# State products taken batch by batch in the layer's layout, and half of a folded weight summed by slices of its contraction

## The chip, the cores and the metric

The kernel runs on one core of one Trainium2 chip. Its metric is the device time of that core in microseconds (us).

## The reference, cut to what matters

```python
# x: (8, 8, 512, 64), state: (8, 8, 32, 64): B, H, S, D and Ns = 32
a     = softmax(scale * x @ state.T)      # over the 32 states
xread = a @ state                         # (B, H, S, D): "x reads state"
a2    = softmax(scale * state @ x.T)      # over the 512 positions
sread = a2 @ x                            # (B, H, Ns, D)
x = concat([xread, sread], axis=2)        # 8 * 544 = 4352 tokens of 512
x = ((x @ w1) * (x @ w2) @ w3) @ w_out    # d_ff 1024, w1 w2 w3 w_out in f64
y = ((x @ wa) * (x @ wb)) @ wo2           # d_ff 1536, the output, f32
```

## The kernel before, in words

The weights come in f64. `load64` brings a raw tile of 512 KB as 32-bit words, and `Convert` makes f32 of it: two ACT activations, a DVE shift and an add on POOL for each raw tile. The SBUF is used as 47 units of 4 KB per partition, and PSUM as 8 banks of 128x512 f32. Products at full width are made in three passes of the f32r type (`PASSES`): every operand is split into a high part (a cast on ACT) and a low part (a subtraction on DVE or POOL), and high x high, high x low and low x high are added in PSUM.

Two products of weights replace work on tokens. First, `w3 @ w_out` is folded once into one 1024x512 weight, `ws`: for each of its eight row blocks, `w3` is loaded by rows, converted, transposed on PE (`transpose_w3`, tiles `w3t`), split and multiplied (`weight_product`, 24 matmuls into a bank `wp`). Second, since xread = a @ state, layer 1 multiplies the attention weights with P = state @ (w1 | w2) of each batch, whose contraction has 256 rows. `state_product` makes P for four batches at once: a matmul takes 64 rows (one head of a pair, r = 0 or 1), 128 columns of the transposed state (4 batches x 32 states) and 512 columns of one of the eight converted weight tiles `wk{p}_{nh}`. Its 64 matmuls fill banks `pb`, ACT or DVE copy them to units `sg` (`product_move`), and `product_store` writes them to DRAM `p_d` in the layer's layout. `load_p` brings one of four chunks of a batch back (`pr`, 512 KB), and `split_p` makes its high part `ph` (ACT) and low part `pl` (POOL, two halves).

The early phase has no order by hand: every operation is a Job with an engine, an estimated time, predecessors and a priority, and `run_jobs` puts them in an order greedily by those estimates; `EARLY` is the order of the loads. In it stand the weight conversions, the folded weight, the attention of batch 0, the state products, and all of layer 1 for batch 0 (`first_product`, tile `f`; `first_output`, tile `x2f`).

Then `block1` runs batches 1 to 7, eight steps `f` each. A step issues on PE: `ap` (6 matmuls) with its copy on ACT; the middle fills; `bp` (6) with the multiplication on DVE and the split into `hp`; the behind fills; and the 12 `x2p` matmuls of the step before. The fills hold the attention of the next batch at fixed steps (`scores` at step 1, for example). The banks in rotation are four, since four more hold the `x2p` sums. The 256 state rows ("s") run interleaved with batch 7, with w1 and w2 loaded a second time by columns (`sw`, 16 loads of 512 KB, and their conversions). Layer 2 (`block2`) follows and isn't touched.

Of the kernel before, what the change touches and what calls it, by code (L numbers as in the profile page):

```python
# [9 lines left out]
F32 = mybir.dt.float32  # L10
F32R = mybir.dt.float32r
# [13 lines left out]
    "wo1 wo3 wo0 w3_1 wo2 w3_2 w3_0 wk0_0 x0 wk1_0 wk2_0 w3_3 "  # L25
    "w3_5 w3_6 x1 wk1_1 w3_4 wk3_0 wk0_1 x2 w3_7 wk3_1 wk2_1"
# [5 lines left out]
KEEP_SG = 2  # L32
KEEP_UNTIL = 40
STORE_BEHIND = 18

LATE_KEEP = 6
LATE_PRIO = 10
# [9 lines left out]
SW_TASKS = 2  # L47
SW_FROM = 46
# [5 lines left out]
P_AHEAD = 3  # L54
# [5 lines left out]
def attention_moe_moe2(  # L60
# [140 lines left out]
    p_d = [dp.tile([2, NP, NS, 2 * DFF1], F32, name=f"p_d{b}") for b in range(B)]  # L201
# [30 lines left out]
    for i in range(NF1):  # L232
        parts[f"w3_{i}"] = rows(w3, i)
    st_s = unit("stT")
# [71 lines left out]
    sg = {}  # L306

    def state_product(p, nh, bg, i):

        for r in range(2):  # L310
            if i == 0:
                sg[p, nh, bg, r] = unit(f"sg{p}_{nh}_{bg}_{r}")
            t = pb[p, nh, bg, i, r] = bank(f"pb{p}_{nh}_{bg}_{i}_{r}")
            rows = slice(r * D, (r + 1) * D)
            nc.tensor.matmul(  # L315
                t,
                lhsT=st_s[rows, (bg * NP + p) * P : (bg * NP + p + 1) * P],
                rhs=conv[f"wk{p}_{nh}"].out[rows, half[i]],
                start=True,
                stop=True,  # L320
            )

    def product_move(p, nh, bg, i, r, eng):
        dst = sg[p, nh, bg, r].rearrange("p (q w c) -> p q w c", q=2, w=2)[:, :, i, :]
        src = flat(pb.pop((p, nh, bg, i, r)), 256)
        if eng == "A":
            nc.scalar.copy(dst, src)
        else:
            nc.vector.tensor_copy(dst, src)

    def product_store(p, nh, bg, r):
        for j in range(4):
            nc.sync.dma_start(
                out=p_d[4 * bg + j][r, p, :, nh * 1024 : (nh + 1) * 1024],
                in_=sg[p, nh, bg, r][j * NS : (j + 1) * NS],
            )
# [12 lines left out]
    wp = {}  # L349

# [324 lines left out]
    def convert_jobs(name):  # L675

        adds = []
        conv[name] = Convert(name, [None, None])
# [21 lines left out]
    def split_jobs(kind, i, name, adds):  # L700
        lows = []
        for k in range(2):
# [7 lines left out]
                prio=1,  # L710
# [7 lines left out]
                    prio=1,  # L718
# [3 lines left out]

    stores = {0: [], 1: []}

    def early_wk(p, nh):
        adds = convert_jobs(f"wk{p}_{nh}")
        last = []
        for bg in range(1):
            moves = {0: [], 1: []}
            for i in range(2):  # L730
                pr = Job(
                    "P",
                    1.0,
                    lambda a=(p, nh, bg, i): state_product(*a),
                    after=[adds[i], state_moved[bg]] + last[-1:],
                    need=2 - 2 * i,
                    keep=KEEP_SG,
                    prio=2 + len(loads) / 100,
                    banks=("ps", 2),
                )  # L740
                last.append(pr)
                for r in range(2):
                    moves[r].append(
                        Job(
                            "AV",
                            (0.6, 0.85),
                            lambda e, a=(p, nh, bg, i, r): product_move(*a, e),
                            after=[pr],
                            prio=0,
                        ).gives("ps", 1)  # L750
                    )
            for r in range(2):
                st = Job(
                    "D",
                    1.5,
                    lambda a=(p, nh, bg, r): product_store(*a),
                    after=moves[r],
                    prio=len(loads) + STORE_BEHIND,
                    lag=2.0,
                ).frees(f"sg{p}_{nh}_{bg}_{r}")  # L760
                if bg == 0:
                    stores[nh].append(st)
        return last
# [45 lines left out]

    wo_done = []  # L810
    products = []
    w_done = []
    for name in EARLY:
        if name[:2] == "wk":
            p, nh = int(name[2]), int(name[4])
            early_wk(p, nh)
        elif name[:2] == "wo":
            i = int(name[2])
            lows = split_jobs("wo", i, name, convert_jobs(name))
            frees_after(lows, name)  # L820
            wo_done += lows
        elif name[:2] == "w3":
# [34 lines left out]

            def result_high(i=i):
                w_s[i] = flat(unit(f"ws{i}", F32R), DM)
                nc.scalar.copy(w_s[i][:, 0, :], wp[i])  # L860

            def result_low(i=i):
                nc.vector.tensor_tensor(
                    out=w_s[i][:, 1, :], in0=wp[i], in1=w_s[i][:, 0, :].bitcast(F32), op=ALU.subtract
                )

            products.append(wpj)
            h = Job("A", 0.6, result_high, after=[wpj], need=1, prio=1)
            w_done.append(Job("V", 0.8, result_low, after=[h], prio=1).gives("ps", 1))
# [173 lines left out]
    sw = Intake("sw", (w1, w2), None, list(range(NF1)))  # L1043
# [269 lines left out]
    last = None  # L1313
    for b, qs in ((0, range(4)), (1, range(3))):
        for q in qs:
            l = Job(
                "D",
                1.5,
                lambda b=b, q=q: load_p(b, q),
                after=stores[q // 2] + ([last] if last else []),  # L1320
                need=1,
                prio=1 + 20 * b,
                lag=1.0,
            )
            if b == 0 or q == 0:
                sp = Job("A", 1.1, lambda b=b, q=q: split_p(b, q), after=[l], need=2, prio=0 + 5 * b)
                ready[b, q] = last = Job("G", 2.4, nothing, after=[sp], prio=0 + 5 * b)
    lows = []
    mults = []
    for f in range(NF1):  # L1330
# [4 lines left out]
            after=[ready[0, f // 2], attended[0][0]],  # L1335
# [10 lines left out]

    last = attended[0][0]
    for p in range(NP):
        for nh in range(2):
            products = []  # L1350
            moves = {0: [], 1: []}
            for i in range(2):
                last = Job(
                    "P",
                    1.0,
                    lambda a=(p, nh, 1, i): state_product(*a),
                    after=[last],
                    need=2 - 2 * i,
                    keep=LATE_KEEP,
                    prio=LATE_PRIO,  # L1360
                    banks=("ps", 2),
                )
                products.append(last)
                for r in range(2):
                    moves[r].append(
                        Job(
                            "A", 0.6, lambda a=(p, nh, 1, i, r): product_move(*a, "A"), after=[last], prio=4
                        ).gives("ps", 1)
                    )
            frees_after(products, f"wk{p}_{nh}")  # L1370
            for r in range(2):
                Job(
                    "D",
                    1.7,
                    lambda a=(p, nh, 1, r): product_store(*a),
                    after=moves[r],
                    prio=len(loads) + STORE_BEHIND,
                    lag=2.0,
                ).frees(f"sg{p}_{nh}_1_{r}")
# [19 lines left out]
    chunks = [(b, q) for b in range(B) for q in range(4)]  # L1399

    for b in range(B):
# [9 lines left out]
        def fills1(f, b=b):  # L1411
            def middle():
                attend(MIDDLE, b, f)
                sw.run(HORIZON[0])
# [368 lines left out]
```

## Time and profile before

| | us |
|---|---|
| median of 3 runs | 1341.95 |
| range of the runs | 1341.14 to 1342.07 |
| profiled execution, device time | 1342.51 |
| its span, first to last instruction | 1340.7 |
| mean granted TensorE clock | 0.988 of full speed |

The profile is of one execution; the span is what its views measure, and the device time is 1.8 us more. PE is TensorE's matmuls, PEld its weight loads, DVE, ACT, POOL and SP the other engines. A timeline shows an instruction's start, its length and, in brackets, the engine's idle time before it and what ended it. Matmuls are pipelined, so the cost of one in a row is the distance between starts and not its length. A line of a group puts equal neighbours together (x12), and an f32 matmul leaves two records, an f32r one a single record.

### The profile page before, as it was taken

What the parts mean: (1) busy time and instruction counts of PE and PEld (TensorE: products, weight loads), DVE (VectorE), ACT (ScalarE), POOL (GpSimd) and SP (SyncE); (2) the same over time, 40 slices, a digit from 0 to 9 for tenths busy, and PEclk for the clock granted to TensorE, in tenths of its full rate; (3) what the DMA queues carried; (4) which work ended last, traced back from release to release, by engine and by line L of the source; (5) the groups of instructions that cost most, each with busy time, mean ns of one, the idle gap of its engine ahead of it and who ended that gap; (6) DMA issues with size and microseconds to landing.
All of it is one profiled execution on the core that took longest, in us unless ns stands there. A gap on an engine that the chain in (4) does not pass through costs nothing.

```text
span 1340.7 us, 17395 instructions
## 1 busy us (share of the span) xinstructions
PE 1300.3 (97%) x6596; PEld 1054.2 (79%) x6596; DVE 612.0 (46%) x792; ACT 550.2 (41%) x951; POOL 439.3 (33%) x352
## 2 busy tenths in 40 slices
PE   3998999999999999999999999999999999999998
PEld 1765768778777789888888888888888888888876
DVE  6676215646666667455532712232722326323240
ACT  7676455655565666354421412211422114221130
POOL 5554214454464477255510430110411103211100
PEclk6999999999999999999999999999999999999999
DMA  9977368493566552777373265542664434744301
GB/s 312 285 234 236 110 205 246 140 290 126 205 205 219 173 174 74 241 269 264 126 267 110 95 215 193 173 149 72 222 218 158 150 115 149 246 173 157 110 0 64
DMA packets 120662, 240.24 MB, mean 179 GB/s; under 512 B 44673, under 2 KB 65153, under 8 KB 120577
## 3 DMA queue, kind: packets, MB, share of 16 engines
q1 hardware_dynamic: 116000, 222.86, 50.5%
q0 software_dynamic: 4576, 16.26, 3.1%
q8 instruction: 52, 0.85, 0.2%
q14 instruction: 34, 0.27, 0.1%
HBM read 173.54 MB, written 65.54 MB: 178 GB/s over the span
## 4 chain that ended last, share of the span: by engine, by line
PE 89%; DMA 4%; DVE 3%; ACT 2%; issue 1%; POOL 1%; SPq 1%; ACTq 0%; POOLq 0%; DVEq 0%
PE r L1497 20%; PE o L1509 19%; PE v L1497 10%; PE x2p L1110 9%; PE bp L1051 5%; PE q L1497 5%; PE ap L1051 5%; PE abs L1552 3%; PE wp L358 2%; PE pb L315 2%; PE x2f L1291 2%; PE f L1051 1%; PE os L1581 1%; PE xt L388 1%; PE bs L1051 1%
## 5 line engine op out<-in xcount | busy, mean ns | idle before, releaser
L1509 PE MATMUL o<-z,h 128*128 128x512 f32 x1152 | 276.6, 389 | 1.3 <-ACT h L136 1.3
L1509 PEld LDWEIGHTS o<-z,h 128*128 128x128 f32 x1152 | 216.1, 188 | 47.0 <-ACT h L136 1.7
L1672 POOL TENSOR_TENSOR hb<-e,e 128x512 f32<-128x512 f32 x48 | 62.9, 1311 | 453.5 <-DVE e L1522 453.4
L136 ACT CAST h<-e 128x512 fp32r<-128x512 f32 x48 | 29.8, 621 | 364.8 <-DVE e L1675 350.8
L1110 PE MATMUL x2p<-hp,ws 128*128 128x512 f32 x672 | 161.9, 390 | 0.0
L1110 PEld LDWEIGHTS x2p<-hp,ws 128*128 128x128 f32 x672 | 125.8, 188 | 26.2
L142 POOL TENSOR_TENSOR pl<-pr,ph 128x512 fp32r<-128x512 f32 x64 | 83.1, 1320 | 120.6 <-ACT ph L136 74.0
L1522 DVE TENSOR_TENSOR e<-e,q 128x512 f32<-128x512 f32 x48 | 33.0, 688 | 195.7 <-PE q L1497 195.7
L1075 DVE TENSOR_TENSOR hfp<-asbp,bp 128x512 f32<-128x512 f32 x56 | 38.3, 684 | 93.6 <-PE bp L1051 89.9
L142 DVE TENSOR_TENSOR hp<-hfp,hp 128x512 fp32r<-128x512 f32 x56 | 54.1, 965 | 40.0 <-ACT hp L136 38.7
L1522 DVE TENSOR_TENSOR e<-e,v 128x512 f32<-128x512 f32 x48 | 33.0, 688 | 85.4 <-PE v L1497 85.4
L1497 PE MATMUL r<-xT2h,w 128*128 128x512 f32 x192 | 67.1, 390 | 0.0
L1497 PE MATMUL r<-xB11h,w 128*128 128x512 f32 x192 | 66.9, 389 | 0.0
L1497 PE MATMUL v<-xT1h,w 128*128 128x512 f32 x192 | 66.9, 389 | 0.0
L1497 PE MATMUL q<-xB21h,w 128*128 128x512 f32 x192 | 66.9, 389 | 0.0
L1497 PE MATMUL r<-xT3h,w 128*128 128x512 f32 x192 | 66.9, 389 | 0.0
L1497 PE MATMUL v<-xB22h,w 128*128 128x512 f32 x192 | 66.9, 389 | 0.0
L1497 PE MATMUL r<-xT4h,w 128*128 128x512 f32 x192 | 66.9, 389 | 0.0
L136 ACT CAST hp<-hfp 128x512 fp32r<-128x512 f32 x56 | 34.7, 620 | 57.0 <-DVE hfp L1075 52.2
L1069 ACT COPY asbp<-ap 128x512 f32<-128x512 f32 x56 | 33.1, 591 | 56.3 <-PE ap L1051 56.2
L142 DVE TENSOR_TENSOR h<-e,h 128x512 fp32r<-128x512 f32 x48 | 35.5, 739 | 33.4 <-ACT h L136 33.4
L1051 PE MATMUL bp<-ah,ph 128*128 128x512 f32 x112 | 47.9, 428 | 1.4 <-DVE a L473 0.9
(476 smaller groups left out, 2815.4 us busy)
## 6 DMA issues: line engine op xcount, KB each, us to landing
w<-w_d SPq DMA_DIRECT2D x168, 512.0 KB, 5.1
w_d<-w SPq DMA_DIRECT2D x48, 512.0 KB, 2.9
p_d<-sg SPq DMA_DIRECT2D x128, 128.0 KB, 2.5
pr<-p_d SPq DMA_DIRECT2D x32, 512.0 KB, 5.2
x<-in_x_dram SPq DMA_DIRECT2D x64, 128.0 KB, 4.6
sw<-in_moe_w_dram SPq DMA_DIRECT2D x16, 512.0 KB, 5.2
xB<-x_d SPq DMA_DIRECT2D x16, 512.0 KB, 4.8
x_d<-x2sp POOLq DMA_DIRECT2D x14, 512.0 KB, 5.8
```

The source lines that it names most:

```text
L136: nc.scalar.copy(hi, src)
L142: (eng or nc.vector).tensor_tensor(out=lo[:, i], in0=src[:, i], in1=hi[:, i].bitcast(F32), op=ALU.subtract)
L315: nc.tensor.matmul(t, lhsT=st_s[rows, (bg * NP + p) * P : (bg * NP + p + 1) * P], rhs=conv[f"wk{p}_{nh}"].out[rows, half[i]], start=True, ...
L1051: nc.tensor.matmul(dst[:, :n], lhsT=l[m], rhs=r[q], start=i == 0 and j == 0, stop=i == k - 1 and j == 2,)
L1069: nc.scalar.copy(a_sb[:, :n], pa[:, :n])
L1075: nc.vector.tensor_tensor(out=hf[:, :n], in0=a_sb[:, :n], in1=pb[:, :n], op=ALU.mult)
L1110: nc.tensor.matmul(acc[j], lhsT=w_s[f][:, m, j * P : (j + 1) * P], rhs=h[:, q, :n], start=per == 1 and f == 0 and i == 0, stop=f == NF1 - ...
L1497: nc.tensor.matmul(t, lhsT=w[m], rhs=xf[g].parts[x][q][:, k, :], start=first and k == 0 and i == 0, stop=k == 1 and i == 2, skip_group_che ...
L1509: nc.tensor.matmul(t, lhsT=h[:, m, part * P : (part + 1) * P], rhs=z_t[f][:, q, :], start=first and c == 0, stop=last and c == 2,)
L1522: nc.vector.tensor_tensor(out=out, in0=x, in1=y, op=ALU.add)
L1552: nc.tensor.matmul(t[:, w * 256 : (w + 1) * 256], lhsT=l[m], rhs=x_s[k][q], start=k == 0 and i == 0, stop=k == 3 and i == 2,)
L1672: nc.gpsimd.tensor_tensor(out=h2[-1][:, f % 2, :], in0=e2, in1=e5, op=ALU.mult)
```

## The change

P is now made for one batch and one chunk at a time. `state_product(b, q)` issues 8 matmuls of 64 rows x 32 columns x 512, which fill two banks already in the layer's layout; `product_high` and `product_low` split them from PSUM straight into `ph` and `pl`. The copies to `sg`, the 128 stores, DRAM `p_d`, the 32 loads and the splits of `pr` are gone. Five of the 32 chunks are made in the early phase, 27 behind steps of layer 1 (`STEPS_P`). The eight `wk` tiles therefore stay in SBUF, and are split in place in batch 7 (`split_weights`) for the state rows, so the second load of w1 and w2 (`sw`) is gone with its conversions.

The folded weight's row blocks 0 to 3 are no longer three-pass products of whole rows. `w3`'s upper half is loaded in eight slices of 256 rows x 512 columns, each transposed, moved as f32 to SBUF and multiplied with the f32 `wo` tile at once; the four banks `wp0` to `wp3` gather four slices of the contraction. Blocks 4 to 7 go as before. The loads stand in another order.

```diff
 EARLY = (
-    "wo1 wo3 wo0 w3_1 wo2 w3_2 w3_0 wk0_0 x0 wk1_0 wk2_0 w3_3 "
-    "w3_5 w3_6 x1 wk1_1 w3_4 wk3_0 wk0_1 x2 w3_7 wk3_1 wk2_1"
+    "wo0 s0 wo1 s1 wo2 s2 x0 wo3 s3 w3_4 wk0_0 w3_5 wk1_0 w3_6 wk2_0 w3_7 "
+    "wk3_0 wk0_1 wk1_1 x1 wk2_1 wk3_1 x2"
 ).split()
...
+STEPS_P = {0: [1], 2: [2], 3: [3], 4: [4]}
+STEPS_P_LAST = ({**STEPS_P, 5: [5]}, {0: [2], 1: [3]})
...
+    for j in range(4):
+        for u in range(2):
+            v = w3[2 * u * P : 2 * (u + 1) * P, j * 512 : (j + 1) * 512]
+            parts[f"s{j}_{u}"] = [v.rearrange("(i p) c -> p i c", p=P)]
...
-    def state_product(p, nh, bg, i):
...
+    def state_product(b, q):
+
+        c = b // 4 * 512 + b % 4 * NS
         for r in range(2):
...
+            pb[b, q, r] = bank(f"pb{b}_{q}_{r}")
+        for p in range(NP):
+            for r in range(2):
+                rows = slice(r * D, (r + 1) * D)
+                w = conv[f"wk{p}_{q // 2}"].out[rows].rearrange("p (w q c) -> p w q c", w=2, q=2)
+                nc.tensor.matmul(
+                    flat(pb[b, q, r], 256)[NS * p : NS * (p + 1)],
+                    lhsT=st_s[rows, c + p * P : c + p * P + NS],
+                    rhs=w[:, :, q % 2, :],
...
+    def product_high(b, q, r):
...
+        nc.scalar.copy(p_s[b, q][0][:, r], flat(pb[b, q, r], 256))
+
+    def product_low(b, q, r):
+        hi, lo = (t[:, r] for t in p_s[b, q])
+        nc.vector.tensor_tensor(
+            out=lo, in0=flat(pb.pop((b, q, r)), 256), in1=hi.bitcast(F32), op=ALU.subtract
+        )
...
+    def slice_product(j, u):
+        wo = flat(conv[f"wo{j}"].out, DM)
+        for i in range(2):
+            if j == 0:
+                wp[2 * u + i] = bank(f"wp{2 * u + i}")
+            for k in range(2):
+                c = (2 * i + k) * P
+                nc.tensor.matmul(
+                    wp[2 * u + i],
+                    lhsT=w3_p[j, u][:, c : c + P],
+                    rhs=wo[:, k, :],
+                    start=j == 0 and k == 0,
+                    stop=j == 3 and k == 1,
+                )
...
+    def split_weights(nh):
+        for k in range(4):
+            hi, lo = unit(f"wkh{k}_{nh}", F32R), unit(f"wkl{k}_{nh}", F32R)
+            split(hi, lo, conv[f"wk{k}_{nh}"].out, ENGINES["VG"[k % 2]])
...
             def behind():
-                if f % 2 == 0:
-                    c = 4 * b + f // 2
-                    if c + 1 < len(chunks):
-                        split_p(*chunks[c + 1])
-                    if c + P_AHEAD < len(chunks):
-                        load_p(*chunks[c + P_AHEAD])
-                        charge(D=1.5)
-                else:
+                if f % 2:
                     free(f"ph{b}_{f // 2}", f"pl{b}_{f // 2}")
                 attend(BEHIND, b, f)
+                for q in slots.get(f, []):
+                    if 4 * b + q < 4 * B:
+                        now[0] += 1.2
+                        state_product(*divmod(4 * b + q, 4))
+                        until[0] = charge(A=1.2, V=1.4)
+                        for r in range(2):
+                            product_high(*divmod(4 * b + q, 4), r)
+                            product_low(*divmod(4 * b + q, 4), r)
+                        until[0] = None
+                if b == B - 1 and f in (0, 2):
+                    split_weights(f // 2)
```

Three places of the built programs, in which a number behind a name is the tile's own. On PE, where the early phase begins, before: `stT` is the transposed state, `w3t` a transposed block of `w3`, `wp1` the first row block.

```order
L264 MATMUL stT1_161<-ident_78,st1_145 128x128 x4
L344 MATMUL w3t1_0_258<-ident_78,w3_1_227 128x128 x4
L344 MATMUL w3t1_1_264<-ident_78,w3_1_227 128x128 x4
L344 MATMUL w3t2_0_298<-ident_78,w3_2_251 128x128 x4
L344 MATMUL w3t2_1_303<-ident_78,w3_2_251 128x128 x4
L358 MATMUL wp1_313<-woh0_215,w3h1_269 128x512
L358 MATMUL wp1_313<-wol0_216,w3h1_269 128x512
```

The same place after: `s0_0` is the first slice, `w3s` its transposes, `w3p` their f32 copy.

```order
L262 MATMUL stT1_153<-ident_78,st1_137 128x128 x4
L355 MATMUL w3s0_0_187<-ident_78,s0_0_175 128x128 x4
L355 MATMUL w3s0_1_200<-ident_78,s0_1_183 128x128 x4
L371 MATMUL wp0_209<-wo0_147,w3p0_0_196 128x512 x2
L371 MATMUL wp1_212<-wo0_147,w3p0_0_196 128x512 x2
L371 MATMUL wp2_235<-wo0_147,w3p0_1_216 128x512 x2
L371 MATMUL wp3_238<-wo0_147,w3p0_1_216 128x512 x2
L355 MATMUL w3s1_0_257<-ident_78,s1_0_227 128x128 x4
```

Products now stand behind one pair of `w3` slices and one `wo` tile, where two row blocks of `w3` and the splits of `wo` stood ahead of them.

On POOL after, in the middle of the early phase: the adds of the last conversions (L177), and `al`, the low part of batch 0's attention weights.

```order
L177 TENSOR_TENSOR w3_5_438<-w3_5_438,w3_5r1_427 128x512
L177 TENSOR_TENSOR wk1_0_491<-wk1_0_491,wk1_0r0_435 128x512
L137 TENSOR_TENSOR al0_637<-a0_598,ah0_636 128x512 x2
L177 TENSOR_TENSOR wk1_0_491<-wk1_0_491,wk1_0r1_447 128x512
L177 TENSOR_TENSOR w3_6_645<-w3_6_645,w3_6r0_471 128x512
```

The adds of `w3_6`, and those of `w3_7` and six `wk` tiles, now stand behind `al`; before, `w3_6` stood ahead of it.

On PE in batch 3, between steps 3 and 4, after: `pb3_3` is the chunk (two banks), and before the change `x2p3_0` followed `bp3_3` at once.

```order
L1049 MATMUL bp3_3_2589<-ah3_2244,pl3_1_2379 128x512
L314 MATMUL pb3_3_0_2610<-wk0_1_735,stT_115 32x512
L314 MATMUL pb3_3_1_2611<-wk0_1_735,stT_115 32x512
L314 MATMUL pb3_3_0_2610<-wk1_1_745,stT_115 32x512
L314 MATMUL pb3_3_1_2611<-wk1_1_745,stT_115 32x512
L314 MATMUL pb3_3_0_2610<-wk2_1_855,stT_115 32x512
L314 MATMUL pb3_3_1_2611<-wk2_1_855,stT_115 32x512
L314 MATMUL pb3_3_0_2610<-wk3_1_865,stT_115 32x512
L314 MATMUL pb3_3_1_2611<-wk3_1_865,stT_115 32x512
L1108 MATMUL x2p3_0_2455<-hp3_2_2513,ws2_518 128x512 x3
```

The chunk has come between; its two banks are taken from the four in rotation until ACT and DVE have read them.

## Rows read from the trace of the kernel before

**Rows 1.** Page: busy us by engine; granted TensorE clock in 40 slices.
```profile
PE 1300.3 (97%) x6596; PEld 1054.2 (79%) x6596; DVE 612.0 (46%) x792; ACT 550.2 (41%) x951; POOL 439.3 (33%) x352
...
PEclk6999999999999999999999999999999999999999
```

**Rows 2.** Waits of PE before 200 us: us in total, times, longest.
```profile
PE w3t L344 <- POOL w L182: 22.3, 6, 14.3
PE f L1051 <- ACT ph L136: 2.3, 2, 1.8
...
PE f L1051 <- POOL pl L142: 1.6, 3, 0.7
```

**Rows 3.** Windows: us, PE busy (x), PEld, DVE, ACT, POOL, PEclk, DMA share, GB/s.
```profile
0.00:190.00 190.00, 160.41 (x796) 109.47 (x797) 97.71 (x129) 124.38 (x230) 77.02 (x64) 0.92 0.74 229
...
10.00:20.00 10.00, 0.00 (x0) 0.00 (x0) 7.44 (x10) 9.52 (x18) 6.73 (x5) 0.50 1.02 391
...
30.00:40.00 10.00, 8.74 (x34) 6.90 (x33) 4.79 (x9) 4.41 (x10) 6.78 (x5) 0.70 1.02 284
...
260.00:400.00 140.00, 139.63 (x856) 111.66 (x855) 85.47 (x107) 82.75 (x145) 75.09 (x63) 1.00 0.64 203
400.00:460.00 60.00, 56.99 (x328) 44.81 (x327) 40.10 (x49) 34.04 (x61) 31.10 (x24) 1.00 0.58 202
```

**Rows 4.** Timelines of PE and POOL, early: start us, us, engine [idle before <-releaser].
```profile
22.96 1.12 PE L344 MATMUL w3t<-ident,w 128*128 128x128 f32 x4 [14.28 <-POOL w L182]
...
12.74 1.29 POOL L182 TENSOR_TENSOR wo<-wo,wo3r 128x512 int32<-128x512 int32 x1 [0.42 <-DVE wo L176]
```

**Rows 5.** Chain of waits: start us, us, engine, tile, line, count.
```profile
40.82 10.90 PE wp L358 x48
```

**Rows 6.** Timeline of PE, end of the early phase.
```profile
173.35 9.71 PE L315 MATMUL pb<-wk,stT 64*128 64x512 f32 x44
182.99 0.50 PE L1051 MATMUL ap<-ah,ph 128*128 128x512 f32 x1
```

**Rows 7.** PE groups over the span: busy us, mean ns | idle before.
```profile
L315 PE MATMUL pb<-wk,stT 64*128 64x512 f32 x128 | 33.7, 615 | 0.3 <-ACT sg L327 0.3
...
L404 PE MATMUL st<-xt,stT 64*32 64x512 f32 x128 | 10.0, 601 | 0.0
```

**Rows 8.** PE timeline: `scores` of batch 2, then two steps.
```profile
187.30 1.09 PE L404 MATMUL st<-xt,stT 64*32 64x512 f32 x16
188.32 0.50 PE L1051 MATMUL bp<-ah,ph 128*128 128x512 f32 x1
...
282.07 2.88 PE L1110 MATMUL x2p<-hp,ws 128*128 128x512 f32 x12
...
286.24 1.09 PE L404 MATMUL st<-xt,stT 64*32 64x512 f32 x16
...
288.75 2.90 PE L1110 MATMUL x2p<-hp,ws 128*128 128x512 f32 x12
...
325.90 2.90 PE L1110 MATMUL x2p<-hp,ws 128*128 128x512 f32 x12
...
331.36 2.88 PE L1110 MATMUL x2p<-hp,ws 128*128 128x512 f32 x12
```

**Rows 9.** Timeline of PE: the first instruction of block 2.
```profile
561.10 0.40 PE L1497 MATMUL r<-xB11h,w 128*128 128x512 f32 x1
```

**Rows 10.** Page, DMA issues: KB each, median us from issue to landing.
```profile
p_d<-sg SPq DMA_DIRECT2D x128, 128.0 KB, 2.5
pr<-p_d SPq DMA_DIRECT2D x32, 512.0 KB, 5.2
```

**Rows 11.** Timelines: ACT's copy of `ap`, a DVE reduction, POOL's early `al`.
```profile
305.55 0.59 ACT L1069 COPY asbp<-ap 128x512 f32<-128x512 f32 x1 [1.97 <-PE ap L1051]
...
297.20 1.21 DVE L420 TENSOR_REDUCE mx<-s 128x2 f32<-128x1024 f32 x1
...
77.73 2.74 POOL L142 TENSOR_TENSOR al<-a,ah 128x512 fp32r<-128x512 f32 x2 [15.07 <-ACT ah L136]
```

More of the change, by code (lines that the diff above doesn't have):

```diff
@@ L305, in attention_moe_moe2 @@
     pb = {}
-    sg = {}
-    def state_product(p, nh, bg, i):
+    def state_product(b, q):
+        c = b // 4 * 512 + b % 4 * NS
         for r in range(2):
[L311 to L327, printed above, removed]
-        else:
[L329 to L336, printed above, removed]
+            pb[b, q, r] = bank(f"pb{b}_{q}_{r}")
[7 more added lines that the diff above has]
+                    rhs=w[:, :, q % 2, :],
+                    start=True,
+                    stop=True,
+                )
+    p_s = {}
+    def product_high(b, q, r):
+        if r == 0:
+            parts = unit(f"ph{b}_{q}", F32R), unit(f"pl{b}_{q}", F32R)
+            p_s[b, q] = [t.rearrange("p (g w c) -> p g w c", g=2, w=2) for t in parts]
+        nc.scalar.copy(p_s[b, q][0][:, r], flat(pb[b, q, r], 256))
[4 more added lines that the diff above has]
+        )
     w3_b = {}
@@ L349, in attention_moe_moe2, with transpose_slice, slice_move @@
     wp = {}
+    w3_p = {}
+    def transpose_slice(j, u):
+        t = w3_b[j, u] = bank(f"w3s{j}_{u}")
+        for k in range(4):
+            part = slice(k * P, (k + 1) * P)
+            nc.tensor.transpose(t[:, part], conv[f"s{j}_{u}"].out[:, part], ident)
+    def slice_move(j, u, eng):
+        w3_p[j, u] = unit(f"w3p{j}_{u}")[:, :512]
+        if eng == "A":
+            nc.scalar.copy(w3_p[j, u], w3_b[j, u])
+        else:
+            nc.vector.tensor_copy(w3_p[j, u], w3_b[j, u])
+    def slice_product(j, u):
[11 more added lines that the diff above has]
+                    stop=j == 3 and k == 1,
+                )
     def weight_product(i):
@@ L677, in convert_jobs @@
         adds = []
-        conv[name] = Convert(name, [None, None])
+        conv[name] = Convert(name, [None] * len(parts[name]))
         for i, v in enumerate(parts[name]):
@@ L698, in state_jobs, with split_jobs @@
             state_moved[bg] = Job("A", 0.65, lambda bg=bg: state_move(bg), after=[t])
-    def split_jobs(kind, i, name, adds):
+    def split_jobs(kind, i, name, adds, prio=1):
         lows = []
@@ L721, in split_jobs @@
         return lows
[L723 to L763, printed above, removed]
     def frees_after(after, *names):
@@ L812, in attention_moe_moe2, with result_jobs, result_high, result_low @@
     w_done = []
+    wo_adds = {}
+    slice_done = {}
+    slices = {j: [] for j in range(4)}
+    def result_jobs(i, product):
+        def result_high():
+            w_s[i] = flat(unit(f"ws{i}", F32R), DM)
+            nc.scalar.copy(w_s[i][:, 0, :], wp[i])
+        def result_low():
+            nc.vector.tensor_tensor(
+                out=w_s[i][:, 1, :], in0=wp[i], in1=w_s[i][:, 0, :].bitcast(F32), op=ALU.subtract
+            )
+        h = Job("A", 0.6, result_high, after=[product], need=1, prio=1)
+        w_done.append(Job("V", 0.8, result_low, after=[h], prio=1).gives("ps", 1))
     for name in EARLY:
         if name[:2] == "wk":
-            p, nh = int(name[2]), int(name[4])
-            early_wk(p, nh)
+            wk_done[int(name[4])] += convert_jobs(name)[-1:]
         elif name[:2] == "wo":
             i = int(name[2])
-            lows = split_jobs("wo", i, name, convert_jobs(name))
-            frees_after(lows, name)
-            wo_done += lows
+            wo_adds[i] = convert_jobs(name)
         elif name[:2] == "w3":
@@ L856, in attention_moe_moe2 @@
             )
[L858 to L865, printed above, removed]
-            products.append(wpj)
-            h = Job("A", 0.6, result_high, after=[wpj], need=1, prio=1)
-            w_done.append(Job("V", 0.8, result_low, after=[h], prio=1).gives("ps", 1))
+            products.append(wpj)
+            result_jobs(i, wpj)
+        elif name[0] == "s":
+            j = int(name[1])
+            for u in range(2):
+                adds = convert_jobs(f"s{j}_{u}")
+                tr = Job("P", 0.5, lambda j=j, u=u: transpose_slice(j, u), after=adds, prio=0, banks=("ps", 1))
+                frees_after([tr], f"s{j}_{u}")
+                mv = Job(
+                    "AV", (0.65, 0.8), lambda e, j=j, u=u: slice_move(j, u, e), after=[tr], need=1, prio=1
+                ).gives("ps", 1)
+                slice_done[u] = Job(
+                    "P",
+                    3.75,
+                    lambda j=j, u=u: slice_product(j, u),
+                    after=[mv, *wo_adds[j], *([slice_done[u]] if j else [])],
+                    prio=1,
+                    banks=("ps", 0 if j else 2),
+                ).frees(f"w3p{j}_{u}")
+                slices[j].append(slice_done[u])
+                if j == 3:
+                    for i in range(2):
+                        result_jobs(2 * u + i, slice_done[u])
+            lows = split_jobs("wo", j, f"wo{j}", wo_adds[j], prio=4)
+            frees_after(lows + slices[j], f"wo{j}")
+            wo_done += lows
         else:
@@ L1312, in attention_moe_moe2 @@
     ready = {}
-    last = None
-    for b, qs in ((0, range(4)), (1, range(3))):
+    for b, qs in ((0, range(4)), (1, range(1))):
         for q in qs:
[L1316 to L1321, printed above, removed]
+            pr = Job(
+                "P",
+                1.2,
+                lambda b=b, q=q: state_product(b, q),
+                after=[*wk_done[q // 2], *state_moved.values()],
                 prio=1 + 20 * b,
-                lag=1.0,
+                banks=("ps", 2),
             )
-            if b == 0 or q == 0:
-                sp = Job("A", 1.1, lambda b=b, q=q: split_p(b, q), after=[l], need=2, prio=0 + 5 * b)
-                ready[b, q] = last = Job("G", 2.4, nothing, after=[sp], prio=0 + 5 * b)
+            ready[b, q] = []
+            for r in range(2):
+                h = Job(
+                    "A",
+                    0.65,
+                    lambda b=b, q=q, r=r: product_high(b, q, r),
+                    after=[pr] + ready[b, q],
+                    need=2 - 2 * r,
+                    prio=5 * b,
+                )
+                ready[b, q].append(
+                    Job("V", 0.75, lambda b=b, q=q, r=r: product_low(b, q, r), after=[h], prio=5 * b).gives("ps", 1)
+                )
     lows = []
@@ L1344, in attention_moe_moe2 @@
         lows.append(lo)
[L1347 to L1379, printed above, removed]
     moves = []
@@ L1396, in attention_moe_moe2 @@
     now[0] = clock["P"]
-    chunks = [(b, q) for b in range(B) for q in range(4)]
+    wk_s = {}
+    def split_weights(nh):
+        for k in range(4):
+            hi, lo = unit(f"wkh{k}_{nh}", F32R), unit(f"wkl{k}_{nh}", F32R)
+            split(hi, lo, conv[f"wk{k}_{nh}"].out, ENGINES["VG"[k % 2]])
+            free(f"wk{k}_{nh}", at=charge(**{"A": 1.1, "VG"[k % 2]: (1.2, 2.7)[k % 2]}))
+            wk_s[k, nh] = hi, lo
     for b in range(B):
@@ L1463, in middle @@
         def middle():
-            sw.run(HORIZON[1])
             ab.run(HORIZON[1])
             if f > 0:
-                xf[0].run(1, keep=8 if sw.next < NF1 else 4)
+                xf[0].run(1, keep=4)
         def behind():
-            free(f"sw{f}h", f"sw{f}l")
-            sw.start(SW_TASKS, reserve=1)
-            if sw.next == NF1 and f >= NF1 - 3:
+            if f % 4 == 3:
+                free(*(f"wk{q}{k}_{f // 4}" for k in range(4) for q in "hl"))
+            if f >= NF1 - 3:
                 ab.start(1, reserve=5)
-            sw.run(HORIZON[1])
             ab.run(HORIZON[1])
-            xf[0].run(1, keep=8 if sw.next < NF1 else 4)
+            xf[0].run(1, keep=4)
             if f >= NF1 - 3 and (0, 0) not in w_t and room(5):
```

46 lines of the change are left out of this document (13 added, 33 removed).

## The prediction

> **What bounds the kernel now.** I read the page first: PE is busy for 97% of the span, and its clock is at full speed but for the start [rows 1]. So a term counts here if it makes PE's stream of instructions longer or shorter, or makes PE idle. The windows tell where PE idles. From 260 to 400 us it is busy 139.63 of 140 us, and from 0 to 190 us 160.41 of 190, which is 29.6 us of idle time [rows 3]. The waits name them: 22.3 us are transposes of `w3` that wait for POOL's add, the last step of a conversion, and 3.9 us are first products of batch 0 that wait for the high and low parts of P [rows 2]. The longest, 14.28 us, is the very first [rows 4]. While PE waits there, the DMAs and ACT are full (share 1.02, 9.52 of 10 us) [rows 3].
>
> So the program has two pieces. An early phase, up to the first matmul of batch 1 at 182.99 us [rows 6], is set by PE's work plus some 30 us of waits. The piece from there to block 2 at 561.10 us [rows 9], 378.1 us, is PE without gaps but for a small one: from 400 to 460 us PE misses 3.0 us [rows 3]. What is moved from the first piece to the second gains its time early and pays it back in full later. Block 2 issues the same work as before, so its 779.6 us stay.
>
> **Part by part.** The sum runs over PE's stream.
>
> *State products taken out of the early phase.* The 64 matmuls of `pb` left 128 records with 33.7 us of busy time [rows 7]. The last block of 22 takes 9.64 us from its first start to that of what follows, where its length says 9.71 [rows 6]; with such overlaps off in all the blocks I take **-33.0 us**.
>
> *The chunks put in.* A chunk is 8 matmuls of 64 rows x 32 columns x 512, f32, which is the form of `scores` [rows 7]. One `scores` takes 1.02 us from its start to that of the next matmul [rows 8]. But the step that holds one lasts 6.68 us (282.07 to 288.75) and one without 5.46 us (325.90 to 331.36) [rows 8]: 1.22 us for the same eight. The 0.20 us between the two numbers lies outside the records, before the first one starts. By the spacing alone the 27 chunks of batches 1 to 7 would cost 27.5 us and the total would be 5.4 us lower; by the steps they cost 32.9. I take the steps, because they hold everything a chunk brings: **+32.9 us**. The five early ones lie between 5.1 and 6.1 us: **+5.5**. The Trainium skill (TensorEngine Tiling (Array Packing), section Key Properties) has a rule that speaks against putting such blocks between full-width ones: changing the tiling mode drains TensorE. The difference of the two steps agrees with it.
>
> *Folded weight, blocks 0 to 3.* Taken out are 4 x 24 passes at 10.90 / 48 = 0.227 us [rows 5], 21.8 us. Put in are 32 f32 matmuls of 128 x 128 x 512. No such one is in the trace. The nearest rows are the f32 matmuls of `pb`, 64 rows high: 9.64 / 22 = 0.438 us each, so 0.876 for the two that make 128 rows [rows 6]. If an f32 matmul of full height takes as long as one of them, the term is 14.0 - 21.8 = -7.8; if it takes as long as two, 28.0 - 21.8 = +6.2. Two records of one f32 matmul against one record of an f32r pass say that it can't be as cheap as a pass, and I take the upper: **+6.2 us**. The Trainium skill (FP8 and Floating Point Precision, section TensorE Precision Notes) says that true FP32 takes four passes through the array; four times 0.227 are an estimate of 0.91 us, by which this term would be +7.3. The transposes are as many as before.
>
> *Waits of the early phase.* Of the old ones 26.2 us go [rows 2]. The first transposes needed the seventh add on POOL; they now need the third. Before, the third began at 12.74 us and took 1.29 [rows 4], so PE can start at 14.1 us and idles 5.4 us ahead of it, not 14.3. Behind that, a slice brings 2 x 4 transposes and 8 products, over 8 us of PE, for four raw tiles, which take ACT 4 x 1.1 us (18 activations and casts in 10 us [rows 3]): conversions run ahead of PE after the first slice, which waits some 1.1 us for its moves. P no longer goes through DRAM, so the waits of `f` end. New ones come in their place. Walking through the new order with the durations of the old rows, I find 9.1 us: 3.0 at the transposes of batch 0's attention, which now come before its exponentials are done, 2.4 at the state reads behind them, 3.7 at the transposes of `w3_6` and `w3_7`, whose adds stand behind `al` on POOL. That `al` takes 2.74 us and can't begin before ACT has cast `ah`, for which POOL idled 15.07 us before [rows 11]. Together 15.6 us of waits for 26.2: **-10.6 us**. With all the 9.1 hidden this is -19.7, with each of them half as long again -6. The clock is 0.50 from 10 to 20 us and 0.70 from 30 to 40 [rows 3], so the first work of PE goes at half speed in either kernel. More work stands there now, which could cost up to 2.4 us more; I count it at nothing, and keep it for the range.
>
> *Waits of the later piece.* A chunk adds two casts on ACT and two subtractions on DVE, and takes from POOL the splits of `pr`. DVE was busy 85.47 of 140 us [rows 3]; two reads of PSUM of about 0.7 us in 27 chunks add 38 us to 378, which leaves it room. But in three batches `bp` of step 4 stands behind a wait for the copy of its own `ap`, 0.59 us on ACT, which it used to run ahead of [rows 11]: 3 x 0.55, **+1.7 us**. Queued behind it on PE is everything. The gaps between 400 and 460 us [rows 3] stood at joints that now have a chunk in them, during which the waited-for engine can finish: I take a third of the 3.0 off, **-1.1**.
>
> *DMAs and other engines.* 128 stores of 128 KB and 32 loads of 512 KB go [rows 10], with the 16 loads of `sw` and their conversions, and eight splits of `wk` come in batch 7. In the later piece PE's idle time is 0.4 us in 140 [rows 3], so no transfer is waited for there, and I cost all of this at **0**. The cover is PE's own work, and it stays.
>
> The sum: -33.0 + 5.5 + 6.2 - 10.6 + 32.9 + 1.7 - 1.1 = **+1.6 us**. Batch 1 begins near 151.1 us instead of 182.99, and the later piece lasts 411.6 us instead of 378.1. The profiled execution took 1342.51 us (span 1340.7 and 1.8 around it), so it would be 1344.1; it lies 0.56 above the median, and on the median's scale the forecast is **1343.5 us**: no change that can be told. A measurement of this kernel tells about 0.2% (2.7 us) from no change.
>
> **Rivals.** *The early phase gets tight* (faster). If the attention chain of batch 0 on ACT and POOL runs before PE asks for it, since raw tiles come at the same pace and POOL has fewer splits, most of the 9.1 us of new waits vanish. That POOL idled 15.07 us ahead of `al` [rows 11] is for it; that the chain depends on ACT, 9.52 of 10 us busy early [rows 3], is against it. Without them 1334.4, with a third of them 1337.4. It decides where `al` ends ahead of the last chunk of folded products.
>
> *PSUM banks turn into a wait* (slower). A chunk holds two of the four rotating banks until DVE's second subtraction. PE has 12 + 6 passes, 18 x 0.227 = 4.1 us [rows 5], before it needs a bank again. Cast, subtract, cast, subtract take about 2.6 us when nothing is ahead of them, but a DVE reduction of the attention takes 1.21 us [rows 11], and the step's own multiplication and split come too. Where two such stand ahead, PE waits some 0.9 us. If that is so in a third of the 27 chunks, it costs 8 us: 1351.5. For it: DVE's reductions begin right behind the steps at which the chunks stand. Against it: `scores` takes two banks in just this way and PE idled only 0.4 us from 260 to 400 us [rows 3].
>
> *An f32 matmul costs as much as one of `pb`* (faster): 14.0 us less, 1329.5. The two records speak against it.
>
> *The eight matmuls of a chunk don't run side by side* (slower): then each pair costs 0.876 us and a chunk 3.5; 32 x 2.3 more give 1417. The same form in `scores` does run side by side [rows 8].
>
> **How the numbers follow.** Forecast 0.42 (1339.5 to 1348), tight early phase 0.29 (1333 to 1339), cheap f32 0.04, bank waits 0.22 (1348 to 1354), chunks in series 0.03. The forecast's case has 0.30 within the 0.2% and 0.12 above it. So faster 0.33, same 0.30, slower 0.37. The range of 1334 to 1352 leaves out the two far cases and the ends of the two near ones, some 0.17.
>
> **What would show it.** Right: the first matmul of batch 1 at 149 to 153 us; slice products 0.85 to 0.95 us apart; a step with a chunk 1.2 us longer than one without; from there to block 2 409 to 414 us. Wrong: waits of `ap` or `bp` for DVE in the steps behind a chunk; no waits ahead of the transposes of `w3_6`; slice products near 0.44 us; chunks near 3.5 us.

## The result, and the profile after

The changed kernel takes **1354.03 us** (median of 4 runs, 1353.01 to 1354.65), the kernel before 1342.01 us beside it (4 runs, 1341.14 to 1343.77). The ratio is 1.0087, with a 95% interval of 1.007 to 1.0105: slower by more than the measurement can miss, and 2 us above the range of the prediction. The profiled execution took 1353.01 us with a span of 1351.2, 10.5 us more than before.

The busy windows of the changed kernel, cut at the first matmul of batch 1 and of block 2 (columns as in [rows 3]):

```profile
0.00:147.65 147.65, 127.40 (x676) 87.19 (x676) 95.99 (x120) 93.83 (x174) 64.43 (x52) 0.95 0.60 189
147.65:562.03 414.38, 411.42 (x2734) 308.98 (x2733) 235.64 (x319) 199.22 (x370) 101.79 (x85) 1.00 0.30 102
562.03:1351.20 789.17, 775.81 (x3542) 645.72 (x3540) 284.70 (x385) 212.32 (x351) 169.74 (x136) 0.99 0.47 162
```

The same three pieces of the kernel before:

```profile
0.00:182.99 182.99, 153.40 (x755) 104.56 (x756) 96.33 (x127) 119.45 (x222) 75.50 (x62) 0.92 0.74 228
182.99:561.10 378.11, 374.43 (x2303) 305.56 (x2302) 228.78 (x283) 220.80 (x383) 197.89 (x156) 1.00 0.60 192
561.10:1340.70 779.60, 772.51 (x3542) 644.03 (x3540) 286.90 (x383) 209.99 (x347) 165.88 (x135) 1.00 0.47 162
```

The early phase is 35.3 us shorter, layer 1 for batches 1 to 7 is 36.3 us longer, and block 2, which issues the same 3542 PE records, is **9.6 us longer**: 13.4 us of it are PE idle instead of 7.1, and the same work is busy 3.3 us longer. The waits of PE in the changed kernel's block 2 (us in total, times, longest) name two places that didn't wait before, when only the last of these three lines had its like (1.3 us):

```profile
PE r L1479 <- ACT e L1619: 6.0, 1, 6.0
PE r L1479 <- DVE e L1504: 1.7, 1, 1.7
PE o L1491 <- ACT h L131: 1.3, 1, 1.3
```

The timelines of ACT and PE there show what holds PE, and one window after it shows the clock:

```profile
675.84 1.04 ACT L131 CAST w<-ab 128x1024 fp32r<-128x1024 f32 x1 [2.73 <-POOL ab L177]
679.73 1.04 ACT L131 CAST w<-ab8s 128x1024 fp32r<-128x1024 f32 x1 [2.85 <-POOL ab8s L957]
...
681.50 0.58 ACT L1619 COPY e<-r 128x512 f32<-128x512 f32 x1
```

```profile
682.13 0.79 PE L1479 MATMUL r<-xT2h,w 128*128 128x512 f32 x1 [5.97 <-ACT e L1619]
...
687.40 0.39 PE L1479 MATMUL q<-xB21h,w 128*128 128x512 f32 x1
```

```profile
682.00:692.00 10.00, 9.87 (x33) 7.92 (x34) 2.43 (x5) 1.43 (x4) 0.00 (x0) 0.73 0.97 350
```

`ab` is the intake of layer 2's weights: column blocks 3 to 8 are loaded and converted while block 2 already runs. The conversion of block `ab8` stands on ACT ahead of the copy that PE needs, and is itself waiting for POOL. PE idles 6 us, and behind the gap the granted clock is 0.73 in the mean of that window: the twelve passes from 682.13 to 687.40 us take 5.27 us, where the same twelve take 2.75 at full clock (643.74 to 646.49 us). The timeline of SP tells when the last six blocks were asked for (only the first of each block's three loads is shown). After:

```profile
550.85 0.38 SPq L889 DMA_DIRECT2D ab<-in_moe_w_b_dram  x1
559.95 0.38 SPq L889 DMA_DIRECT2D ab<-in_moe_w_b_dram  x1
593.95 0.43 SPq L889 DMA_DIRECT2D ab<-in_moe_w_b_dram  x1
606.09 1.39 SPq L889 DMA_DIRECT2D ab<-in_moe_w_b_dram  x1
630.34 0.38 SPq L889 DMA_DIRECT2D ab<-in_moe_w_b_dram  x1
650.98 0.39 SPq L889 DMA_DIRECT2D ab<-in_moe_w_b_dram  x1
```

Before:

```profile
530.39 0.37 SPq L890 DMA_DIRECT2D ab<-in_moe_w_b_dram  x1
554.12 0.38 SPq L890 DMA_DIRECT2D ab<-in_moe_w_b_dram  x1
586.22 0.67 SPq L890 DMA_DIRECT2D ab<-in_moe_w_b_dram  x1
600.90 0.39 SPq L890 DMA_DIRECT2D ab<-in_moe_w_b_dram  x1
618.88 0.71 SPq L890 DMA_DIRECT2D ab<-in_moe_w_b_dram  x1
646.70 0.39 SPq L890 DMA_DIRECT2D ab<-in_moe_w_b_dram  x1
```

Block 2 starts within 1 us at the same time in both, yet `ab3` is asked for 20 us later, `ab7` 11 us and `ab8` 4 us. The code says why: behind steps 5 to 7 of the state rows `ab.start(1, reserve=5)` wants 6 + 5 units of SBUF free. By the planner's own count 14 were free at step 5 before. After, it counts 10 at steps 5 and 6 and 17 at step 7: the split of the `wk` tiles is not in place, as the section on the change has it; each takes two new units (`wkh`, `wkl`) and gives one back, and the eight units of the second four tiles stay until step 7.

### The profile page after: what moved, and what is told of

It is laid out like the page before. It is cut to its first block, busy times and chain, and to the rows that moved or that the text cites. A ratio compares the mean times of both kernels' runs of the same rounds, so it can differ in the third digit from the quotient of the medians.

```text
span 1351.2 us, 17636 instructions
## 1 busy us (share of the span) xinstructions
PE 1314.6 (97%) x6948; PEld 1041.9 (77%) x6948; DVE 616.3 (46%) x823; ACT 505.4 (37%) x895; POOL 336.0 (25%) x273
## 4 chain that ended last, share of the span: by engine, by line
PE 88%; DVE 5%; ACT 3%; issue 1%; DMA 1%; POOL 1%; SPq 0%; POOLq 0%; DVEq 0%; ACTq 0%
PE o L1491 19%; PE r L1479 19%; PE x2p L1108 10%; PE v L1479 9%; PE bp L1049 5%; PE ap L1049 5%; PE q L1479 5%; PE abs L1534 2%; PE pb L314 2%; PE f L1049 2%; PE x2f L1289 2%; PE wp L371 2%; PE os L1563 1%; PE bs L1049 1%; PE as L1049 1%
## 5 line engine op out<-in xcount | busy, mean ns | idle before, releaser
L1108 PE MATMUL x2p<-hp,ws 128*128 128x512 f32 x672 | 165.6, 395 | 0.0
L137 DVE TENSOR_TENSOR hp<-hfp,hp 128x512 fp32r<-128x512 f32 x56 | 44.3, 792 | 40.3 <-ACT hp L131 40.3
L1067 ACT COPY asbp<-ap 128x512 f32<-128x512 f32 x56 | 32.9, 587 | 73.7 <-PE ap L1049 73.5
L177 POOL TENSOR_TENSOR ab<-ab,ab 128x512 int32<-128x512 int32 x24 | 31.5, 1333 | 73.7 <-ACT asbp L1067 33.3
```

The costliest lines, as they stand in the source:

```text
L137: (eng or nc.vector).tensor_tensor(out=lo[:, i], in0=src[:, i], in1=hi[:, i].bitcast(F32), op=ALU.subtract)
L177: nc.gpsimd.tensor_tensor(out=out, in0=out, in1=d.bitcast(I32), op=ALU.add)
L1067: nc.scalar.copy(a_sb[:, :n], pa[:, :n])
L1108: nc.tensor.matmul(acc[j], lhsT=w_s[f][:, m, j * P : (j + 1) * P], rhs=h[:, q, :n], start=per == 1 and f == 0 and i == 0, stop=f == NF1 - ...
```

## The experiments

**The start of the intake, in the changed kernel (e1_ab_room).**

```diff
-                ab.start(1, reserve=5)
+                ab.start(1, reserve=4)
```

> The changed kernel with one constant different: behind steps 5 to 7 of the state rows the intake of layer 2's weights may begin with 10 SBUF units free instead of 11. Theory (room): the eight split wk tiles leave 10 units at step 5, one too few, so the load of column block ab3 began at 551 us instead of 530, every later block followed late, and PE waited 7.7 us for ab7 and ab8 in block 2 and ran at half clock behind the longer wait. Then ab3 is issued near 535 us, the waits of r in block 2 go, block 2 takes 779 to 781 us as before the change and not 789.2, and the kernel takes 1344 to 1346 us. Rival (block 2's own queues are slower after the change, whatever the start of ab3): block 2 stays above 786 us and the kernel at 1352 to 1355.

Measured: 1343.18 us (10 runs, 1342.6 to 1343.9) beside 1343.77 for the kernel before (13 runs), ratio 1.0003 (0.9993 to 1.0012); 0.8 us below the range that I had expected. `ab3` is asked for at 525.99 us, 9 us earlier than I expected, the two waits of `r` are gone from block 2, and its window is

```profile
562.55:1340.80 778.25, 772.62 (x3542) 644.13 (x3540) 288.61 (x383) 209.90 (x348) 167.71 (x136) 1.00 0.47 165
```

One unit of reserve gives back the whole loss. The rival falls: nothing else in block 2 had become slower.

**The same delay, in the kernel before (e2_before_late).**

```diff
-            if sw.next == NF1 and f >= NF1 - 3:
+            if sw.next == NF1 and f >= NF1 - 1:
                 ab.start(1, reserve=5)
```

> The kernel before, with the intake of layer 2's weights held back from step 5 to step 7 of the state rows and nothing else. Theory (room): a late ab3 alone makes the loss, so the kernel before gets the waits of r in block 2 too: block 2 787 to 790 us instead of 779.6, the kernel 1350 to 1352 us. Rival (the loss needs the changed kernel's split weights or its queues): block 2 stays within 1 us of 779.6 and the kernel at 1342.

Measured: 1353.55 us (4 runs, 1350.81 to 1354.27), ratio 1.0077 (1.0057 to 1.0096); 1.6 us above the range that I had expected. `ab3` is asked for at 540.95 us, 10.6 us later than before. Block 2's window, and its new waits of PE:

```profile
559.81:1349.00 789.19, 775.03 (x3542) 645.37 (x3540) 284.81 (x385) 212.38 (x351) 169.80 (x136) 1.00 0.46 159
```

```profile
PE r L1497 <- ACT e L1637: 6.0, 1, 6.0
PE r L1497 <- DVE e L1522: 1.7, 1, 1.7
```

The same two waits, of the same length, in a kernel that has nothing of the change. The late start alone makes the loss.

**State products alone (e3_no_slices).** The load order of before, `w3` by rows, and the splits of `wo` where they were:

```diff
-    "wo0 s0 wo1 s1 wo2 s2 x0 wo3 s3 w3_4 wk0_0 w3_5 wk1_0 w3_6 wk2_0 w3_7 "
-    "wk3_0 wk0_1 wk1_1 x1 wk2_1 wk3_1 x2"
+    "wo1 wo3 wo0 w3_1 wo2 w3_2 w3_0 wk0_0 x0 wk1_0 wk2_0 w3_3 "
+    "w3_5 w3_6 x1 wk1_1 w3_4 wk3_0 wk0_1 x2 w3_7 wk3_1 wk2_1"
...
-            wo_adds[i] = convert_jobs(name)
+            lows = split_jobs("wo", i, name, convert_jobs(name))
+            frees_after(lows, name)
+            wo_done += lows
```

> The changed kernel with the folded weight and the load order of before: state products batch by batch alone. Theory: PE's early work falls by 33.0 and grows by 5.7 for five chunks, and the waits of f for the chunks from DRAM (3.9 us) go, while the waits for w3 (22.3 us) and the slow clock until 35 us stay: batch 1 begins at 151 to 154 us, so the slices are worth 4 to 6 us, most of it clock and the first wait, since their f32 products cost 5.7 us more than the three passes. From there on as the changed kernel (414 and 789 us): 1357 to 1360 us. Rival (the slices gain nothing, the early phase is shorter for the products alone): batch 1 at 147 to 149 us and 1353 to 1355.

Measured: 1356.13 us (4 runs, 1355.45 to 1356.81), ratio 1.0098 (1.0078 to 1.0119). Its early window:

```profile
0.00:151.43 151.43, 123.15 (x707) 94.80 (x708) 94.80 (x126) 95.23 (x177) 62.10 (x51) 0.90 0.59 184
```

Batch 1 begins at 151.43 us, as the theory had it, so the products alone are worth 31.6 us early and the slices with their load order 3.8 in the two profiles, and 2.1 between the medians: less than the 4 to 6 I gave them. From there it takes 414.35 and 789.12 us, as the changed kernel does. The slices add 4.3 us to PE's busy time (127.40 against 123.15) and take 8.0 off its idle time.

**Every chunk twice (e4_twice).**

```diff
-                        state_product(*divmod(4 * b + q, 4))
+                        state_product(*divmod(4 * b + q, 4), times=2)
```

(`times` repeats the eight matmuls.)

> The changed kernel with the eight matmuls of each of the 27 chunks of batches 1 to 7 issued twice, into the same banks. A chunk made a step 1.11 to 1.4 us longer, where its eight matmuls take 1.02 us from start to start within the block. Theory (a fixed price of some 0.25 us for going into the 64 x 32 form and out of it): the second eight add 1.02 us each, 27.5 us in all, and the steps with a chunk grow by 1.0 to 1.05. Rival (the eight themselves cost 1.27 us beside full-width matmuls): 27 x 1.27 = 34.3 us.

Measured: 1375.78 us (one run), 21.8 us more than the changed kernel's median. Both numbers I had expected are too high. The timeline of PE at a chunk with sixteen matmuls, between its start and that of the next `x2p`:

```profile
206.30 1.95 PE L314 MATMUL pb<-wk,stT 64*32 64x512 f32 x32
208.18 3.01 PE L1108 MATMUL x2p<-hp,ws 128*128 128x512 f32 x12
```

The same place with eight, in the changed kernel:

```profile
196.69 2.90 PE L1108 MATMUL x2p<-hp,ws 128*128 128x512 f32 x12
202.25 1.09 PE L314 MATMUL pb<-wk,stT 64*32 64x512 f32 x16
203.26 3.03 PE L1108 MATMUL x2p<-hp,ws 128*128 128x512 f32 x12
210.09 2.90 PE L1108 MATMUL x2p<-hp,ws 128*128 128x512 f32 x12
```

The second eight add 1.88 - 1.01 = 0.87 us; 27 of them make 23.5 us. From batch 1 to block 2 the profile takes 22.2 us more: the four blocks that stretch in the changed kernel (see the later piece below) take 1.88 us here like the others, and one other takes 2.79. In the changed kernel the step that holds a chunk takes 6.57 us (196.69 to 203.26) where it took 5.45 before, and the one behind it 6.83 (to 210.09) where it took 6.68, both without a listed wait: a chunk costs 1.12 + 0.15 = 1.27 us. Of that, 0.87 are the eight matmuls and 0.40 the way into the other form and out of it, a part of it behind the chunk. The Trainium skill (TensorEngine Tiling (Array Packing), section Key Properties) says that a change of tiling mode drains TensorE. The 0.40 agrees with that, but no run tells the drain from anything else that the change of form brings.

**Two blocks joined (e5_joined).**

```diff
-STEPS_P = {0: [1], 2: [2], 3: [3], 4: [4]}
+STEPS_P = {0: [1], 3: [3], 4: [4]}
...
                 attend(MIDDLE, b, f)
+                if f == 1 and 0 < b < B - 1:
+                    chunk(2)
```

(`chunk` is the loop's body as a function; the constant of e1_ab_room is in it.)

> As e1_ab_room, with chunk 2 of batches 1 to 6 moved from behind step 2 into step 1, right behind the scores of the next batch, so that the two blocks of the 64 x 32 form share one way in and one way out. Theory (0.41 us of a chunk's 1.27 are the way in and out, 0.86 its eight matmuls, as the doubled chunks showed): step 2 becomes 1.12 us shorter and the step after it 0.14, step 1 becomes 0.86 longer, 6 x 0.40 = 2.4 us less in all: the piece from batch 1 to block 2 lasts 411.9 us instead of 414.3, the kernel 1340.8 us. Rival (banks: the scores hold two of the four rotating banks and the chunk two more, so the chunk or bp of step 1 waits for the copies on ACT): waits of pb or bp of 0.4 us and more in each of the six, and nothing gained, 1343 to 1345.

Measured: 1340.59 us (10 runs, 1338.73 to 1341.18), ratio to the kernel before 0.9984 (0.9975 to 0.9993); 2.6 us less than e1_ab_room. Here the kernel before took 1342.69 us and beside e1_ab_room 1343.77; by the two ratios the difference is 2.6 us as well. From batch 1 to block 2 it takes 560.11 - 149.06 = 411.05 us instead of 414.33. The joined blocks:

```profile
204.31 3.03 PE L1108 MATMUL x2p<-hp,ws 128*128 128x512 f32 x12
208.63 1.09 PE L432 MATMUL st<-xt,stT 64*32 64x512 f32 x16
209.51 1.06 PE L314 MATMUL pb<-wk,stT 64*32 64x512 f32 x16
...
212.00 2.88 PE L1108 MATMUL x2p<-hp,ws 128*128 128x512 f32 x12
```

Behind `scores` the chunk makes its step 7.69 us (204.31 to 212.00), 0.86 more than without it, and no bank is waited for. The theory holds for the joined blocks; the piece got 3.3 us shorter where 2.4 were expected, and the rest isn't assigned.

**The w3 loads ahead (e6_w3_first).**

```diff
-    "wo0 s0 wo1 s1 wo2 s2 x0 wo3 s3 w3_4 wk0_0 w3_5 wk1_0 w3_6 wk2_0 w3_7 "
-    "wk3_0 wk0_1 wk1_1 x1 wk2_1 wk3_1 x2"
+    "wo0 s0 wo1 s1 wo2 s2 x0 wo3 s3 w3_4 w3_5 w3_6 w3_7 wk0_0 wk1_0 wk2_0 "
+    "wk3_0 wk0_1 wk1_1 x1 wk2_1 wk3_1 x2"
```

> As e1_ab_room, with the loads of w3_4 to w3_7 all ahead of the wk tiles. Theory (the wait of 2.1 to 3.5 us ahead of the transposes of w3_6 is POOL's: its adds stand behind al): with the adds of w3_6 and w3_7 ahead of al that wait goes, and as the chunks need all of the wk tiles only 20 us later nothing takes its place: batch 1 begins at 144.5 to 146.5 us instead of 148.2, the kernel takes 1340 to 1342 us. Rival (the wk tiles become the late ones): the w3 wait goes, and a new one stands ahead of pb or of f; batch 1 at 148 us or later, 1343 us or more.

Measured: 1337.56 us (4 runs, 1336.78 to 1338.3), ratio 0.9958 (0.9943 to 0.9973). Batch 1 begins at 143.90 us. PE's early waits for POOL and ACT, besides the first slices:

```profile
PE pb L314 <- POOL wk L177: 1.9, 1, 1.9
PE a2t L491 <- ACT e L458: 1.8, 1, 1.8
```

The wait for `w3_6` is gone, and so is the one of the state reads; a wait for `wk` has come, as the rival had it, but of 1.9 us only. Both mechanisms act, and the gain is 5.6 us to e1_ab_room's median where I had 1 to 3; in the two profiles it is 4.3, all of it ahead of batch 1.

**Both edits (e7_both).**

> As e1_ab_room, with both edits, the joined chunk and the w3 loads ahead. If both theories hold: 2.4 + 2.5 us less than e1_ab_room, 1338 to 1339.5 us, faster than either kernel. If either rival holds, 1341 to 1343.

Measured: **1334.06 us** (5 runs, 1333.27 to 1334.93), ratio to the kernel before 0.9935 (0.9923 to 0.9948). That is better than I had expected, because e6_w3_first was: the two gains as measured, 2.6 and 5.6 us off 1343.18, give 1335.0. With one unit less in reserve, one load order and one moved chunk, the change is faster than the kernel before by 0.5 to 0.8%.

## Why the prediction was wrong

**The step that failed** is "Block 2 issues the same work as before, so its 779.6 us stay". The work is the same, but the time at which its weights arrive is not: the intake of layer 2's weights starts behind the last steps of layer 1, if enough SBUF units are free. I had written that "eight splits of `wk` come in batch 7" and costed them by the engines' time alone, at 0. They also hold 8 units of SBUF until step 7 of the state rows, and that left 10 free at step 5 where the intake wants 11. e1_ab_room takes the delay away and lands at 1343.18 us where 1343.5 was forecast. That it comes so close is in part luck: without the delay the early phase is still 2.9 us shorter than forecast and the later piece 2.7 us longer. e2_before_late brings the delay into the kernel before and costs it the same two waits. Of the 9.6 us, PE's idle time in block 2 is 6.3 (13.4 less 7.1), and 2.5 are the twelve passes at the slower clock behind the gap; 0.8 more of busy time isn't assigned. None of my rivals had this mechanism; the range missed it by 2 us.

**State products out, chunks in.** The chunk costs 1.27 us and not 1.22, since it delays the first `x2p` behind it as well: 27 x 1.27 = 34.3 for 32.9. Going by the steps and not by the spacing was right.

**The later piece.** +36.3 us where I had 33.5. Besides 1.4 for the chunks it is the rival of the banks, in part. Four chunk blocks, at step 4 of three batches and step 5 of one, stretch from 1.09 us to 1.29, 1.68 (twice) and 2.01, since a bank that they need is still being read. PE shows it as busy time:

```profile
231.64 1.68 PE L314 MATMUL pb<-wk,stT 64*32 64x512 f32 x16
```

```profile
228.46 1.21 DVE L471 TENSOR_REDUCE m<-t 128x32 f32<-128x1024 f32 x1
229.70 1.22 DVE L472 TENSOR_TENSOR t<-t,m 128x1024 f32<-128x1024 f32 x1
230.84 0.16 DVE L402 RECIPROCAL r<-r 128x2 f32<-128x2 f32 x1
230.92 1.27 DVE L332 TENSOR_TENSOR pl<-pb,ph 128x512 fp32r<-128x512 f32 x2
```

Two DVE operations of the attention stand ahead of the subtractions of the chunk before, just as the rival said, but in four of the 27 chunks, for 2.3 us together and not 8. The wait of `bp` for its own copy came as forecast, 1.7 us in three batches. PE's idle time fell by 0.7 us in this piece, where I took off 1.1 and put on 1.7. That is 1.4 + 2.3 - 1.3 = 2.4 of the 2.8 us; the rest is open.

**The folded weight.** The f32 products stand in the groups of PE, early, as

```profile
L371 PE MATMUL wp<-wo,w3p 128*128 128x512 f32 x64 | 29.1, 604 | 0.3 <-DVE w3p L362 0.3
```

Eight of them from 33.97 to 40.84 us make 0.859 us each; I took 0.876 of a range from 0.438. The upper bound was the right choice. The four passes that the Trainium skill (FP8 and Floating Point Precision, section TensorE Precision Notes) gives to true FP32 agree: the estimate of 0.91 us from them is 6% high.

**The early phase.** Batch 1 began at 147.65 us, 3.5 us before my 151.1. The first transposes started at 14.78 us (forecast 14.1). The waits that I had walked through came where I put them: `a2t` 2.6 us (forecast 3.0), the state reads 2.5 (2.4), `w3_6` and `w3_7` 2.1 and 0.9 (3.7), and the idle time fell from 29.6 to 20.2 us, by 9.3 (10.6). What I had not counted is 4.7 us more off PE's busy time: it fell by 26.0 us, where the counted work falls by 33.0 - 5.5 - 6.2 = 21.3. e3_no_slices splits it: without the slices 2.8 of it are there already (30.2 less 27.5), and 1.9 come with them (4.3 added for 6.2).

The 2.8 can't be the clock of the start, since e3_no_slices starts as the kernel before does and has the lower mean clock (0.90 for 0.92). Its `f` products are busy 37.6 us, and 39.7 before. Before, they waited for P, and behind the waits ran slowly in these windows, seven passes in 3.06 us (128.54 to 131.60) where seven take 1.6 at full clock:

```profile
128.00:130.00 2.00, 1.46 (x4) 1.05 (x5) 2.00 (x3) 1.76 (x4) 2.00 (x3) 0.52 0.02 8
130.00:132.00 2.00, 2.00 (x7) 1.63 (x7) 1.97 (x2) 1.29 (x2) 2.00 (x2) 0.63 0.43 136
```

That is 1.5 of the 2.8; with P from PSUM neither the waits nor the slow stretch is there. The 1.9 do fit the clock of the start. e3_no_slices runs four groups of `w3` transposes (1.11 us for 0.60 at full clock) and six passes (2.71 us for 1.36) slowly, which loses 3.4 us; the changed kernel two groups and its first eight slice products (7.35 us for 6.87), which loses 1.5. No run changed the clock alone, so all this is read from rows and not shown by an experiment. I had kept up to 2.4 us for it on the other side.

**The transfers** that went were worth little or nothing, as forecast: layer 1's DMA share fell from 0.60 to 0.30, and PE's idle time there from 3.7 to 3.0 us.

## What to carry to other kernels

A change that holds buffers longer is not costed by its instructions: list what starts only when that many buffers are free, and follow it into the next stage, since there the same work can come late. Where a planner decides by a threshold, compare its count on both sides; here 10 against 11 units cost 9.6 us, and one constant brought them back. And small blocks of another matmul form pay a fixed price each, here 0.40 us of 1.27, so put them next to each other.

## What the runs showed of the hardware

Eight f32 matmuls of 64 rows x 32 columns, side by side, add 0.87 us, which is what one f32 matmul of 128 x 128 takes (0.859): a packed block moves at the pace of a full one.

A granted clock of 1.00 in a window isn't always the pace of TensorE. From 10 to 20 us the changed kernel and e4_twice, whose early programs are alike, show 0.58 and 1.00:

```profile
10.00:20.00 10.00, 4.63 (x13) 2.78 (x14) 6.66 (x10) 9.32 (x18) 6.00 (x5) 0.58 1.02 389
```

```profile
10.00:20.00 10.00, 4.87 (x12) 2.92 (x13) 6.80 (x10) 9.22 (x18) 6.24 (x5) 1.00 1.04 395
```

The first eight slice products begin there (x16, two records each). In the changed kernel and in e4_twice they stand, with the transposes behind them, as

```profile
17.39 7.51 PE L371 MATMUL wp<-wo,w3p 128*128 128x512 f32 x16
24.74 1.04 PE L355 MATMUL w3s<-ident,s 128*128 128x128 f32 x8
```

```profile
17.16 8.63 PE L371 MATMUL wp<-wo,w3p 128*128 128x512 f32 x16
25.63 1.04 PE L355 MATMUL w3s<-ident,s 128*128 128x128 f32 x8
```

Eight take 6.87 us at full clock, 7.35 in the changed kernel and 8.47 in e4_twice, the one that shows 1.00; in e1_ab_room and e5_joined, which show 0.51 and 0.50, they take 8.15 and 8.76. Their first transposes take 1.11 or 1.12 us in all four, where such a group takes 0.60 later. So the first work ran at half clock in all four, and the 1.00 is no fast start: e4_twice's trace has no record of the clock before 20.38 us, and a stretch without one reads as full. What differs is when the clock rose: at 18.4 us in the changed kernel, 19.8 in e1_ab_room, 21.2 in e5_joined, and by the record that begins there 20.4 in e4_twice. Batch 1 begins at 147.65, 148.22, 149.06 and 148.50 us, in the same order. Why the rise comes at different times is open; no run was made for it.
